# Attention by pairs of heads in the halves of TensorE's rows

## The chip, the cores and the metric

The kernel runs on one core of a Trainium2 chip. The metric is the device time of one execution in microseconds. Engines are named as the profile names them: PE (TensorE, matmuls), PEld (its weight loads), DVE (VectorE), ACT (ScalarE), POOL (GpSimd) and SP (SyncE, which issues nearly all DMAs).

## What is computed

Three layers follow each other. Attention with a sigmoid in place of the softmax: 4 batches, 12 heads, 448 tokens, 64 values per head. Then a dense block with 768 inputs and 2048 hidden values (ELU). Then a mixture of 8 experts, in which a greedy assignment gives each expert 224 tokens.

```
scores = scale * np.matmul(q, k.transpose(0, 1, 3, 2)) - np.log(S)
attn = 1.0 / (1.0 + np.exp(-scores))
x = np.matmul(attn, v)                      # (4, 12, 448, 64) -> rows of 768
h = x @ w_in
x2 = np.where(h > 0.0, h, np.exp(np.minimum(h, 0.0)) - 1.0) @ w_out
logits = x2 @ w_gate                        # greedy choice, 224 tokens an expert
out[mask] = np.maximum(x2[mask] @ w1[e], 0.0) @ w2[e]
```

## The kernel before

**Precision.** Most matmuls work on float32r operands that are split in two: a high part (a copy that rounds, `hcopy`, on ACT or DVE) and a low part (the rest, a subtraction on DVE, `lsub`). A product is then high by high, high by low and low by high: three matmuls, one "group of three". Products with v are plain float32 matmuls; the trace shows each as two MATMUL instructions.

**Attention** (`attention`, L452). For each head the host lays k and q transposed and twice below each other: 64 rows and the same 64 rows again. `prep` (L442) makes `kk`, whose upper half is the high part of k and whose lower half the low part, and `qh` and `ql`, the high and the low part of q in both halves. One matmul of `kk` with `qh` over all 128 rows then gives high by high and low by high at once, a second one with `ql` the rest: two matmuls of 448 columns per head and chunk of 112 keys. The result lies in one of three PSUM banks (`sc`); ACT applies the sigmoid, one instruction per head and chunk, into one of eight tiles `s`. Products with v follow four (head, chunk) steps later, in one unit per chunk in batch 0 (`AC0`) and per two chunks later (`AC1`): the two heads of a pair write partitions 0 to 63 and 64 to 127 of one bank (`av`). After four chunks the pair's output is split into `xH` and `xL`, one tile each for the six pairs of a batch.

**Dense block.** `layer1` (L496) makes 16 tiles of hidden values, each with six groups of three into one of four banks (`mm`), and then the epilogue: exp and tanh on ACT, two DVE operations that read the bank, and the split into `gH` and `gL`. `layer2` (L519) makes six output tiles of 16 groups of three each, in the first three of these banks; the fourth (`lg`) collects the logits. `rows_out` (L575) transposes a finished tile in an `sc` bank and stores it. In batch 0 the weights come as wide integers, and `weights` (L417) turns them into float32 with three DVE operations and one of ACT before the split; later batches read the copy that it has stored.

**Order.** A planner (`Plan`) writes the whole order before the kernel runs. Every operation has a cost and a rank by place in the program; the planner takes, engine by engine, what can start first, and the lower rank among ties. Units (`plan.unit`) of matmuls stay together. Work that depends on data waits for the ends that the planner has computed; on the chip each engine keeps this order. The program order is attention 0, then for each batch `layer1(b)`, `attention(b + 1)`, `layer2(b)`. A sigmoid needs another table of ACT than exp and tanh, and the planner counts 1.3 us for a change.

After the dense block come the search (counting matmuls and DVE operations in `search`), the lists, gathers and the experts, which use all eight banks under new names.

Of the kernel before, what the change touches and what calls it, by code (L numbers as in the profile page):

```python
# [18 lines left out]
MM = 4  # L19
PC = 1  # L20
XLA = 4
NK = 4
NA_ = 8
AV = 7
PP = 2
NR = 3
# [26 lines left out]
class Plan:  # L53
# [39 lines left out]
    @staticmethod  # L93
    def region(ap):
        steps = list(ap.ap)
        size = mybir.dt.size(ap.dtype)
        name = ap.tensor.name
        if ap.tensor.__class__.__name__ == "Tile" and ap.space != bass.MemoryType.DRAM:
            if ap.space == PSUM:
                return name, 0, 128, 0, 2048  # L100
            row = steps[0][0]
            p0, off = divmod(ap.offset, row) if row else (0, ap.offset)
            span = 1 + sum((n - 1) * s for s, n in steps[1:])
            return name, p0, p0 + steps[0][1], off * size, (off + span) * size
        span = 1 + sum((n - 1) * s for s, n in steps)
        return name, 0, 1, ap.offset * size, (ap.offset + span) * size
# [180 lines left out]
def kernel(  # L287
# [11 lines left out]
    B, H, D2, S = kq.shape  # L299
    S, D = S // 2, D2 // 2  # L300
    NT, DM = out.shape
# [82 lines left out]
    xH = p1.tile([P, KD, S], F32R)  # L384
    xL = p1.tile([P, KD, S], F32R)
# [11 lines left out]
    heads = {}  # L397

    def load_head(h):
        if h >= B * H or h in heads:  # L400
            return
        b, hh = divmod(h, H)
        x = r_kq()
        if h == 0:
            for c in (slice(0, S), slice(S, 2 * S)):
                plan.dma(x[:, c], kq[b, hh][:, c])
        else:
            plan.dma(x, kq[b, hh])
        vr = None
        if hh % 2 == 0:  # L410
            vr = r_v()
            plan.dma(vr.rearrange("p c d -> p (c d)"), vP[b, hh // 2])
        heads[h] = (x[:, :S], x[:, S:], vr)
# [28 lines left out]
    def prep(h, st):  # L442
        kr, qr, vr = heads[h]
        kk, qh, ql = r_kk(), r_qh(), r_ql()
        hcopy(kk, kr)
        lsub(kk[D:], kr[D:], kk[D:])
        hcopy(qh, qr)
        lsub(ql, qr, qh)
        st[h] = (kk, qh, ql, vr)
        load_head(h + 2)  # L450

    def attention(b):  # L452
        st, ad = {}, {}
        n0, n1 = b * H * C, (b + 1) * H * C
        LA = XLA
        AC = AC0 if b == 0 else AC1

        def scores(n):
            g, r = divmod(n, 2 * C)
            c, j = divmod(r, 2)  # L460
            h = 2 * g + j
            if n < n0 + 2:
                prep(h, st)
            if c == PP + j and g + 1 < (b + 1) * (H // 2):
                prep(h + 2, st)
            kk, qh, ql, _ = st[h]
            ps = sc()
            with plan.unit():
                for i, m in enumerate((qh, ql)):
                    PE.matmul(ps[:CP, :S], kk[:, c * CP:(c + 1) * CP], m, start=i == 0, stop=i == 1)  # L470
            ad[n] = r_s()[:CP]
            A.activation(ad[n], ps[:CP, :S], AF.Sigmoid, bias=bias_s[:CP], scale=QS)

        for n in range(n0, n1 + LA):
            if n < n1:
                scores(n)
            m = n - LA
            if m < n0 or (m + 1) % (2 * AC):
                continue
            g, r = divmod(m, 2 * C)  # L480
            c = r // 2
            if c == AC - 1:
                ps = av()
            v = st[2 * g][3]
            with plan.unit():
                for i in range(AC):
                    for j in range(2):
                        o, k = slice(j * D, (j + 1) * D), c - AC + 1 + i
                        PE.matmul(ps[o, :S], v[:, k, o], ad.pop(m + 1 - 2 * (AC - i) + j), start=k == 0,
                                  stop=k == C - 1)  # L490
            if c == C - 1:
                hp = g % (H // 2)
                hcopy(xH[:, hp, :], ps[:, :S])
                lsub(xL[:, hp, :], ps[:, :S], xH[:, hp, :])

    def layer1(b):  # L496
        ws = {}
        for f in range(-2, KF):
            with plan.first(200), plan.after(xH[:, GW + f]) if b == 0 and f < 1 else nullcontext():
                if f + 2 < KF:  # L500
                    ws[f + 2] = weights(b, f + 2)
# [4 lines left out]
            for c in range(KD):  # L506
                with plan.unit():
                    for n, (w, m) in enumerate(((h, xH), (h, xL), (l, xH))):
                        PE.matmul(ps[:, :S], w[:, c, :], m[:, c, :], start=c == 0 and n == 0,
# [9 lines left out]
    def layer2(b):  # L519
        ws = {}  # L520
        m3 = Ring(banks[:MM - 1])

# [7 lines left out]
        for d in range(KD):  # L530
# [10 lines left out]
            x2, xh, xl = r_s() if b == B - 1 else r_x2(), r_x2h(), r_x2l()  # L541
            last = b == B - 1 and d == KD - 1
            with plan.first(3000):
# [11 lines left out]
                if d == KD - 1:  # L555
# [3 lines left out]
                    pl = sc()[:, :(j1 - j0) * 2 * E]  # L559
# [15 lines left out]
    def rows_out(b, d, x2, e):  # L575
        rows, pr = r_rows(), sc()
# [7 lines left out]
    load_head(0)  # L584
    load_head(1)
# [119 lines left out]
    def search(parts, n=1):  # L705
# [8 lines left out]
        for i, (nb, sh) in enumerate(BITS):  # L714
# [33 lines left out]
            if lead:  # L748
                warm(W1, banks[3], full[:K])
# [30 lines left out]
    mm, sc, av = Ring(banks[:3]), Ring(banks[3:7]), Ring(banks[7:])  # L780
# [24 lines left out]
    def listing(ph):  # L805
# [8 lines left out]
        if ph == 0:  # L814
            warm(W4, banks[3], csb)
# [19 lines left out]
        if ph == 0:  # L835
            warm(W3, banks[3], idx)
# [167 lines left out]
```

## Time and profile before

| | before |
|---|---|
| median of three runs | 1052.14 us (1050.41 to 1054.1) |
| profiled execution | 1051.52 us |
| its span, first to last instruction | 1049.6 us |
| mean granted clock of PE in it | 0.973 |
| attention 0 and layer 1 of batch 0 | 0 to about 149 us |
| layer 2 of batch 0, attention 1 | about 149 to 250 us |
| batches 1 to 3 | about 250 to 700 us |
| search and experts | from about 700 us |

The span is what the rows below count from. Matmuls are pipelined: the start of one to the start of the next is what it costs, its own duration is longer. A mean of a group is of one instruction.

### The profile page before, as it was taken

Reading aid. Unit: us, or ns where it says so; the run is one execution under the profiler, and the core shown is the slowest. Engines: PE = TensorE matmul, PEld = TensorE weight load, DVE = VectorE, ACT = ScalarE, POOL = GpSimd, SP = SyncE. Lnnn points to the kernel's source line nnn. Section 1 sums busy time; section 2 is a strip of 40 time slices with the busy share of each in tenths; the row PEclk is TensorE's granted clock in tenths of the full one; section 3 lists DMA queues with packets and bytes.
Section 4 is the critical chain, followed back from the end, with each engine's and each line's share of the span. In section 5 each row is a group of like instructions: output and inputs, shape, how many; then the busy total and the mean of one; then the engine's idle time right before and its main releaser. Section 6 shows DMA issues by size and latency. Waiting matters only on the chain. (4 is left out here: it accounts for less than half of the span.)

```text
span 1049.6 us, 15479 instructions
## 1 busy us (share of the span) xinstructions
PE 997.6 (95%) x5810; PEld 837.4 (80%) x5810; DVE 752.7 (72%) x1446; ACT 453.2 (43%) x790; POOL 44.5 (4%) x43
## 2 busy tenths in 40 slices
PE   8998879999999999999999999978969999999997
PEld 3466755789985788995698999955969999899997
DVE  5878987867885545995244995448788898898871
ACT  5887657743357402347412331024244453353330
POOL 0000000000000000000000000001021121020200
PEclk9998989999999999999999999996989999999999
DMA  6785766664335433334133333126255375375830
GB/s 204 266 299 211 231 242 257 202 238 147 114 125 178 138 117 103 111 132 156 29 113 102 106 126 104 58 53 236 108 217 203 146 239 203 120 266 193 296 100 26
DMA packets 54058, 170.89 MB, mean 163 GB/s; under 512 B 6112, under 2 KB 17120, under 8 KB 52448
## 3 DMA queue, kind: packets, MB, share of 16 engines
q1 hardware_dynamic: 51424, 158.90, 44.4%
q0 software_dynamic: 2560, 11.01, 3.3%
q8 instruction: 45, 0.74, 0.3%
q14 instruction: 29, 0.24, 0.1%
HBM read 146.30 MB, written 23.59 MB: 162 GB/s over the span
## 5 line engine op out<-in xcount | busy, mean ns | idle before, releaser
L246 PE MATMUL bank<-xH,wh 128*128 128x448 f32 x384 | 143.6, 374 | 11.1 <-DVE a L246 9.9
L246 PE MATMUL bank<-x,eh 128*128 128x224 f32 x768 | 141.4, 287 | 5.9 <-ACT x L246 3.2
L246 PE MATMUL bank<-gH,wh 128*128 128x448 f32 x384 | 142.1, 370 | 0.0
L246 PE MATMUL bank<-xL,wh 128*128 128x448 f32 x384 | 141.7, 369 | 0.0
L246 PE MATMUL bank<-xH,wl 128*128 128x448 f32 x384 | 141.5, 369 | 0.0
L246 PE MATMUL bank<-gH,wl 128*128 128x448 f32 x384 | 140.6, 366 | 0.0
L246 PE MATMUL bank<-gL,wh 128*128 128x448 f32 x384 | 140.4, 366 | 0.0
L246 PEld LDWEIGHTS bank<-x,eh 128*128 128x128 f32 x768 | 120.8, 197 | 8.0 <-ACT x L246 3.7
L246 DVE TENSOR_TENSOR wl<-wd,wh 128x768 fp32r<-128x768 f32 (+1 forms) x112 | 119.6, 1070 | 9.4 <-ACT wh L246 4.6
L246 DVE TENSOR_TENSOR el<-eraw,eh 128x768 fp32r<-128x768 f32 x128 | 121.0, 950 | 3.7 <-ACT eh L246 2.9
L246 ACT ACTIVATE s<-bank,bias_s 112x448 f32<-112x448 f32 x192 | 110.6, 635 | 28.0 <-PE bank L246 24.4
L246 DVE CAST wh<-wd 128x768 fp32r<-128x768 f32 (+1 forms) x83 | 51.3, 618 | 91.9 <-PE bank L246 88.7
L246 ACT ACTIVATE eh<-eraw 128x768 fp32r<-128x768 f32 x106 | 85.9, 842 | 70.1 <-DMA eraw<-we 57.8
L246 ACT ACTIVATE a<-bank 128x448 f32<-128x448 f32 x128 | 66.1, 541 | 105.8 <-PE bank L246 99.5
L246 PE MATMUL bank<-x,el 128*128 128x224 f32 x384 | 107.0, 279 | 0.0
L246 PEld LDWEIGHTS bank<-xH,wh 128*128 128x128 f32 x384 | 73.1, 190 | 23.2 <-issue 10.8
L246 PE MATMUL bank<-eh,hH 128*112 128x384 f32 x256 | 88.6, 346 | 0.0
L246 PE MATMUL bank<-eh,hL 128*112 128x384 f32 x256 | 86.3, 337 | 0.0
L246 PE MATMUL bank<-el,hH 128*112 128x384 f32 x256 | 86.2, 337 | 0.0
L246 PE MATMUL bank<-s,vr 112*64 112x448 f32 x384 | 84.5, 557 | 0.0
L246 PE MATMUL bank<-qh,kk 128*112 128x448 f32 x192 | 75.8, 395 | 8.1 <-DVE kk L246 6.6
L246 PEld LDWEIGHTS bank<-gH,wh 128*128 128x128 f32 x384 | 72.2, 188 | 11.0 <-issue 3.5
(143 smaller groups left out, 1597.1 us busy)
## 6 DMA issues: line engine op xcount, KB each, us to landing
eraw<-we SPq DMA_DIRECT2D x64, 768.0 KB, 5.3
kq<-kq SPq DMA_DIRECT2D x47, 448.0 KB, 4.0
wd<-wcopy SPq DMA_DIRECT2D x48, 384.0 KB, 2.9
wd<-wcopy SPq DMA_DIRECT2D x36, 512.0 KB, 3.2
arena<-w_in SPq DMA_DIRECT2D x16, 768.0 KB, 5.3
arena<-w_out SPq DMA_DIRECT2D x12, 1024.0 KB, 8.4
wcopy<-wd SPq DMA_DIRECT2D x16, 384.0 KB, 4.9
wcopy<-wd SPq DMA_DIRECT2D x12, 512.0 KB, 4.2
```

Source lines behind the costliest of these rows:

```text
L246: fn = lambda: getattr(self.eng[e], name)(*args, **kw)
```

## The change

Pairs of heads take the place of single heads. The host lays the two heads of a pair below each other (64 rows each), so that k and q are loaded once and not twice. `prep` splits a pair with one copy and one subtraction over 896 columns (k and q side by side). The scores of a chunk are a group of three for each head, each over 64 rows: head 0 in rows 0 to 63, head 1 in rows 64 to 127, taken in turn; they go to the two banks of a "twin" tile, and one sigmoid reads both. PSUM has two twins, one `av` bank and three `mm` banks (four before); `layer2` has two of these (three before), and the logits have the third. From batch 1 on, the scores of two chunks and the products with v of the two chunks before them are one unit ("one stretch"); in batch 0 they stay apart. The output of a pair goes to a ring of nine tiles each for the high and the low part. The costs of the planner follow the new shapes, and PSUM regions are told apart by bank, as a twin has two.

```diff
-MM = 4
+MM = 3
-XLA = 4
-NK = 4
-NA_ = 8
-AV = 7
+XLA = 2
+NK = 2
+NA_ = 4
+XT = 3
...
-            if ap.space == PSUM:
-                return name, 0, 128, 0, 2048
...
+            if ap.space == PSUM:
+                return name, 0, 128, off // 512, (off + span + 511) // 512
...
-            if ins[0].dtype == F32R and out.shape[0] == 64:
-                return 0.121
+            if ins[0].dtype == F32R and ins[0].shape[0] == 64:
+                return 0.104
...
-    banks = [psum.tile([P, 512], F32, name=f"bank{i}") for i in range(8)]
-    mm, sc, av = Ring(banks[:MM]), Ring(banks[MM:AV]), Ring(banks[AV:])
+    banks = [psum.tile([P, 512], F32, name=f"bank{i}") for i in range(4)]
+    twins = [psum.tile([P, 2, 512], F32, name=f"twin{i}") for i in range(2)]
+    mm, sc, av = Ring(banks[:MM]), Ring(twins), Ring(banks[MM:])
...
-    r_v = ring(p1, "vr", [CP, C, P], F32, 3)
-    r_kk = ring(p1, "kk", [P, S], F32R, NK)
-    r_qh = ring(p1, "qh", [P, S], F32R, NK)
-    r_ql = ring(p1, "ql", [P, S], F32R, NK)
+    r_v = ring(p1, "vr", [CP, C, P], F32, 4)
+    r_kqh = ring(p1, "kqh", [P, 2 * S], F32R, NK)
+    r_kql = ring(p1, "kql", [P, 2 * S], F32R, NK)
-    r_s = ring(p1, "s", [P, S], F32, NA_)
+    r_s = ring(p1, "s", [P, 2, S], F32, NA_)
...
-    xH = p1.tile([P, KD, S], F32R)
-    xL = p1.tile([P, KD, S], F32R)
+    r_xH = ring(p1, "xH", [P, S], F32R, KD + XT)
+    r_xL = ring(p1, "xL", [P, S], F32R, KD + XT)
+    xs = [[] for _ in range(B)]
...
-    def prep(h, st):
-        kr, qr, vr = heads[h]
-        kk, qh, ql = r_kk(), r_qh(), r_ql()
-        hcopy(kk, kr)
-        lsub(kk[D:], kr[D:], kk[D:])
-        hcopy(qh, qr)
-        lsub(ql, qr, qh)
-        st[h] = (kk, qh, ql, vr)
-        load_head(h + 2)
+    def prep(g, st):
+        x, vr = pairs[g]
+        h, l = r_kqh(), r_kql()
+        for c in (slice(0, S), slice(S, 2 * S)) if g == 0 else (slice(0, 2 * S),):
+            hcopy(h[:, c], x[:, c])
+            lsub(l[:, c], x[:, c], h[:, c])
+        st[g] = (h[:, :S], l[:, :S], h[:, S:], l[:, S:], vr)
+        load_pair(g + 2)
...
         def scores(n):
+            g, c = divmod(n, C)
+            kh, kl, qh, ql, _ = st[g]
             ps = sc()
+            for i, (w, m) in enumerate(((kh, qh), (kh, ql), (kl, qh))):
+                for j in range(2):
+                    o = slice(j * D, (j + 1) * D)
+                    PE.matmul(ps[:CP, j, :S], w[o, c * CP:(c + 1) * CP], m[o], start=i == 0, stop=i == 2)
+            return ps
+
+        def values(n):
+            g, c = divmod(n, C)
+            if c == 0:
+                acc[g] = av()
+            v, s = st[g][4], ad.pop(n)
+            for j in range(2):
+                o = slice(j * D, (j + 1) * D)
+                PE.matmul(acc[g][o, :S], v[:, c, o], s[:, j], start=c == 0, stop=c == C - 1)
+
+        for n in range(n0, n1 + XLA, AC):
+            new = [i for i in range(n, n + AC) if i < n1]
+            old = [i for i in range(n - XLA, n - XLA + AC) if i >= n0]
...
             with plan.unit():
+                pss = [scores(i) for i in new]
+                if b:
+                    for i in old:
+                        values(i)
+            if not b and old:
+                with plan.unit():
+                    for i in old:
+                        values(i)
+            for i, ps in zip(new, pss):
+                ad[i] = r_s()[:CP]
+                A.activation(ad[i], ps[:CP, :, :S], AF.Sigmoid, bias=bias_s[:CP], scale=QS)
...
+                h, l = r_xH(), r_xL()
...
-    mm, sc, av = Ring(banks[:3]), Ring(banks[3:7]), Ring(banks[7:])
+    mm, sc, av = Ring(banks[:3]), Ring([t[:, i] for t in twins for i in range(2)]), Ring(banks[3:])
...
+    kt, qt = (x.transpose(0, 1, 3, 2).reshape(B, H // 2, 2 * D, S) for x in (k, q))
...
-        "kq": np.concatenate([dup(k), dup(q)], axis=3), "vP": vp,
+        "kq": np.concatenate([kt, qt], axis=3), "vP": vp,
```

The warm-up matmuls of the search move from the fourth bank to the third, which is then the logits' one, and layer 2 of the last batch keeps its six results in three of the double `s` tiles.

## Rows read from the trace of the kernel before

**Rows 1.** The page's totals: busy us (share of the span) xinstructions.

```profile
PE 997.6 (95%) x5810; PEld 837.4 (80%) x5810; DVE 752.7 (72%) x1446; ACT 453.2 (43%) x790; POOL 44.5 (4%) x43
```

**Rows 2.** Busy time by stretch: us, each engine (instructions), clock, DMA, GB/s.

```profile
0.00:12.70 12.70, 7.73 (x23) 3.81 (x23) 7.24 (x29) 5.64 (x9) 0.43 (x5) 0.92 0.71 200
12.70:82.00 69.30, 68.72 (x301) 37.74 (x300) 50.99 (x78) 53.89 (x95) 0.00 (x0) 0.99 0.78 271
82.00:93.00 11.00, 6.29 (x17) 4.70 (x17) 9.76 (x16) 10.30 (x18) 0.00 (x0) 0.69 0.88 313
93.00:109.50 16.50, 16.50 (x81) 14.86 (x80) 14.47 (x23) 11.67 (x21) 0.00 (x0) 1.00 0.40 133
109.50:149.00 39.50, 28.81 (x129) 24.73 (x128) 35.47 (x51) 22.30 (x35) 0.00 (x0) 0.91 0.70 240
149.00:250.00 101.00, 99.87 (x494) 77.06 (x493) 74.42 (x108) 60.08 (x94) 0.62 (x3) 1.00 0.64 223
250.00:600.00 350.00, 350.00 (x1722) 287.14 (x1722) 226.05 (x378) 138.21 (x254) 0.00 (x0) 1.00 0.37 117
```

The engines in these rows are PE, PEld, DVE, ACT and POOL. Eleven of the 23 matmuls before 12.7 us are warm-up matmuls ahead of the first scores.

**Rows 3.** Timeline of PE in attention 0: start, us, what, xcount.

```profile
31.32 0.46 PE L246 MATMUL bank<-qh,kk 128*112 128x448 f32 x1
31.61 0.37 PE L246 MATMUL bank<-ql,kk 128*112 128x448 f32 x1
31.91 0.97 PE L246 MATMUL bank<-s,vr 112*64 112x448 f32 x4
32.81 0.46 PE L246 MATMUL bank<-qh,kk 128*112 128x448 f32 x1
...
47.19 1.72 PE L246 MATMUL bank<-s,vr 112*64 112x448 f32 x8
```

**Rows 4.** Timeline of PE at the start; in brackets the idle time before.

```profile
4.73 0.43 PE L246 MATMUL bank<-qh,kk 128*112 128x448 f32 x1
...
9.57 0.46 PE L246 MATMUL bank<-qh,kk 128*112 128x448 f32 x1 [3.40 <-DVE kk L246]
```

**Rows 5.** Timeline of PE from 82 to 149 us.

```profile
85.30 0.45 PE L246 MATMUL bank<-qh,kk 128*112 128x448 f32 x1 [3.21 <-DVE kk L246]
...
143.39 0.71 PE L246 MATMUL bank<-xH,wh 128*128 128x448 f32 x1 [5.23 <-DVE a L246]
```

**Rows 6.** Groups by shape, whole span: xcount, busy us, mean ns, idle before.

```profile
L246 ACT ACTIVATE s<-bank,bias_s 112x448 f32<-112x448 f32 x192 | 110.6, 635 | 28.0 <-PE bank L246 24.4
L246 PE MATMUL bank<-s,vr 112*64 112x448 f32 x384 | 84.5, 557 | 0.0
...
L246 PE MATMUL bank<-ql,kk 128*112 128x448 f32 x192 | 71.8, 374 | 1.4 <-DVE ql L246 1.3
...
L246 DVE TENSOR_TENSOR wl<-wd,wh 128x768 fp32r<-128x768 f32 x64 | 61.1, 955 | 5.0 <-ACT wh L246 2.0
L246 DVE TENSOR_TENSOR wl<-wd,wh 128x1024 fp32r<-128x1024 f32 x48 | 58.6, 1222 | 4.4 <-ACT wh L246 2.6
...
L246 DVE TENSOR_TENSOR ql<-kq,qh 128x448 fp32r<-128x448 f32 x48 | 29.9, 624 | 1.1
L246 DVE TENSOR_TENSOR kk<-kq,kk 64x448 fp32r<-64x448 f32 x48 | 29.9, 623 | 3.1 <-ACT kk L246 1.7
...
L246 ACT ACTIVATE wh<-wd 128x768 fp32r<-128x768 f32 x18 | 15.1, 845 | 10.9 <-PE bank L246 10.9
...
L246 ACT ACTIVATE wh<-wd 128x1024 fp32r<-128x1024 f32 x11 | 11.6, 1057 | 12.5 <-PE bank L246 9.0 <-DVE wd L246 3.5
```

**Rows 7.** Timeline of PE in the expert stage, two places three weight loads apart.

```profile
861.08 0.27 PE L246 MATMUL bank<-x,el 128*128 128x224 f32 x1
...
861.41 0.28 PE L246 MATMUL bank<-x,el 128*128 128x224 f32 x1
```

**Rows 8.** DMA issues: xcount, KB each, us to landing.

```profile
kq<-kq SPq DMA_DIRECT2D x47, 448.0 KB, 4.0
```

**Rows 9.** Busy time by stretch, instructions that touch `xH` alone.

```profile
12.70:82.00 69.30, 15.87 (x48) 9.01 (x48) 3.73 (x6) 3.29 (x6) 0.99 0.78 271
```

More of the change, by code (lines that the diff above doesn't have):

```diff
@@ L395, with load_pair @@
     Lm = const.tile([P, NJ, E], F32)
-    heads = {}
-    def load_head(h):
-        if h >= B * H or h in heads:
+    pairs = {}
+    def load_pair(g):
+        if g >= B * HP or g in pairs:
             return
-        b, hh = divmod(h, H)
-        x = r_kq()
-        if h == 0:
+        b, hp = divmod(g, HP)
+        x, vr = r_kq(), r_v()
+        if g == 0:
             for c in (slice(0, S), slice(S, 2 * S)):
-                plan.dma(x[:, c], kq[b, hh][:, c])
+                plan.dma(x[:, c], kq[b, hp][:, c])
         else:
[L408 to L413, printed above, removed]
+            plan.dma(x, kq[b, hp])
+        plan.dma(vr.rearrange("p c d -> p (c d)"), vP[b, hp])
+        pairs[g] = (x, vr)
     wcopy = dram.tile([KF + 2 * KD, P, KH, P], F32, name="wcopy") if wide else None
@@ L452, in attention @@
     def attention(b):
         st, ad = {}, {}
-        n0, n1 = b * H * C, (b + 1) * H * C
-        LA = XLA
+        n0, n1 = b * HP * C, (b + 1) * HP * C
         AC = AC0 if b == 0 else AC1
+        acc = {}
         def scores(n):
[L459 to L466, printed above, removed]
-            ps = sc()
-            with plan.unit():
[L469 to L494, printed above, removed]
+            g, c = divmod(n, C)
@@ new lines, in attention @@
+        for n in range(n0, n1 + XLA, AC):
+            new = [i for i in range(n, n + AC) if i < n1]
+            old = [i for i in range(n - XLA, n - XLA + AC) if i >= n0]
+            for i in new:
+                g, c = divmod(i, C)
+                if i == n0:
+                    prep(g, st)
+                if c == PP and g + 1 < (b + 1) * HP:
+                    prep(g + 1, st)
+            with plan.unit():
+                pss = [scores(i) for i in new]
[9 more added lines that the diff above has]
+                A.activation(ad[i], ps[:CP, :, :S], AF.Sigmoid, bias=bias_s[:CP], scale=QS)
+            if old and old[-1] % C == C - 1:
+                h, l = r_xH(), r_xL()
+                ps = acc.pop(old[-1] // C)
+                hcopy(h, ps[:, :S])
+                lsub(l, ps[:, :S], h)
+                xs[b].append((h, l))
@@ L498, in layer1 @@
         for f in range(-2, KF):
-            with plan.first(200), plan.after(xH[:, GW + f]) if b == 0 and f < 1 else nullcontext():
+            with plan.first(200), plan.after(xs[0][GW + f][0]) if b == 0 and f < 1 else nullcontext():
                 if f + 2 < KF:
@@ L507, in layer1 @@
                 with plan.unit():
-                    for n, (w, m) in enumerate(((h, xH), (h, xL), (l, xH))):
-                        PE.matmul(ps[:, :S], w[:, c, :], m[:, c, :], start=c == 0 and n == 0,
+                    for n, (w, m) in enumerate(((h, 0), (h, 1), (l, 0))):
+                        PE.matmul(ps[:, :S], w[:, c, :], xs[b][c][m], start=c == 0 and n == 0,
                                   stop=c == KD - 1 and n == 2)
@@ L521, in layer2 @@
         m3 = Ring(banks[:MM - 1])
+        keep = [r_s() for _ in range(KD // 2)] if b == B - 1 else None
         def fetch(i):
@@ L575, in rows_out @@
     def rows_out(b, d, x2, e):
-        rows, pr = r_rows(), sc()
+        rows, pr = r_rows(), sc()[:, 0]
         with plan.unit() if b < B - 1 else nullcontext():
@@ L583 @@
     late = []
[L584 to L585 removed]
+    load_pair(0)
+    load_pair(1)
     V.memset(bias_s, -math.log(S))
@@ L748, in search @@
             if lead:
-                warm(W1, banks[3], full[:K])
+                warm(W1, banks[2], full[:K])
             V.tensor_reduce(out=num if last else dlt, in_=nums, axis=AX.X, op=ALU.max)
@@ L814, in listing @@
         if ph == 0:
-            warm(W4, banks[3], csb)
+            warm(W4, banks[2], csb)
         V.tensor_reduce(out=s2, in_=sp_.rearrange("p (x j) -> p j x", x=2), axis=AX.X, op=ALU.min)
@@ L835, in listing @@
         if ph == 0:
-            warm(W3, banks[3], idx)
+            warm(W3, banks[2], idx)
         xg = []
```

10 lines of the change are left out of this document (4 added, 6 removed).

## The prediction

> **What bounds the kernel now.** I read the totals first [rows 1]: TensorE is busy for 95% of the span, VectorE for 72%, ScalarE for 43%. A share over the whole span says little here, so the next view is busy time by stretch [rows 2]. Its stretches are cut where the work changes: the start (0 to 12.7 us), attention of batch 0 (to 82), the changeover to layer 1 of batch 0 (to 93), the rest of that layer (to 149), then layer 2 of batch 0 with attention of batch 1 (to 250). From 250 to 600 TensorE is busy for 350.0 of 350 us at full clock: whatever TensorE is spared there comes off the time, and what ScalarE or VectorE is spared does not, as they are busy for 138 and 226 us. Before 149 it is otherwise. From 93 to 109.5 us the rows show 81 matmuls in 16.5 us, 0.204 us each; that is the price of one 448-column float32r matmul at full clock. At this price the 12 score matmuls between the first one (4.73 us [rows 4]) and 12.7 are 2.4 us of work in 8.0, the 17 between 82 and 93 are 3.5 in 11, and the 129 from 109.5 to 149 are 26.3 in 39.5. The three stretches lose 5.5, 7.5 and 13.2 us: 26 us in which TensorE stands, or runs at the lower clock (means of 0.92, 0.69 and 0.91).
>
> The timeline says what it stood for. At the start it is the second head: the first has its scores by 6 us, the next score matmul waits 3.40 us for that head's `kk` [rows 4]. At 85.30 it is again `kk`, at 143.39 the layer-1 epilogue on VectorE (`a`, 5.23 us) [rows 5]. From 109.5 to 149 VectorE is busy for 35.5 of 39.5 us [rows 2]: the conversion of the weights of batch 0 and the epilogues set the pace there, not TensorE.
>
> **The scores.** There are 96 pair-chunks (4 batches, 6 pairs of heads, 4 chunks). Each now takes four matmuls over 128 rows (192 + 192 in all; [rows 6] has one half), 0.815 us. The change takes six over 64 rows, two at a time in the two halves. If the halves run side by side this is three times 0.204 = 0.611 us, a gain of 0.204 per chunk, 19.6 us for 96. If they run one after the other it is six times 0.204, a loss of 39.2 us. These are the two ends. No row shows row halves. The nearest are the products with v, whose outputs lie in the two column halves: each MATMUL has a mean of 557 ns against 374 for the float32r one [rows 6], yet four of them more in one stretch add only 1.72 - 0.97 = 0.75 us [rows 3], 0.19 each. So an instruction that streams for two passes (557 - 374 = 183 ns more, one pass) is issued every single pass: two are in flight at a time, in different halves. The weights don't forbid it: in the expert stage three loads of 128 columns are taken every 0.33 us (861.08 to 861.41 [rows 7]), 0.11 each, while six loads of 112 columns have 0.611 us here. I take the near end, -19.6 us, with a chance kept for the far one.
>
> The Trainium skill, "TensorE: Matmul & The Clock Gate", section "The mechanism", says that matmuls in different row groups overlap and start some 4 ns apart. By that figure, an estimate, 288 pairs would cost 1.2 us more; no run so far shows it.
>
> **The changes of mode.** A visit to the column halves isn't free. From the `qh` matmul at 31.32 to the next at 32.81 [rows 3] are 1.49 us; two score matmuls (0.41) and four value matmuls (0.75) leave 0.33 us for going in and coming out. In batches 1 to 3 this visit exists 36 times (12 per batch, two chunks each), before and after. What is new is a third change: layer matmuls, row halves, column halves, layer matmuls. Its cost is between 0 and a whole visit, 0.33 us; a half is nearest, 0.17, or 6.1 us for 36 (bounds 0 and 12). In batch 0, where scores and products with v alternate already, the row halves take the place of the full array on one side; where a layer-1 group stands between, a change is added. I take 1 us (0 to 4).
>
> This is where a rule speaks against the change. The Trainium skill, "TensorEngine Tiling (Array Packing)", section "Key Properties", says that changing the mode, not only the tile, drains TensorE. It gives no price; the 0.33 us above agree with it, and by it the third change is certain to cost something.
>
> **What the other engines are spared.** Splitting now takes, for each head, two subtractions of 0.62 us (48 each in the trace) and two copies; for a pair that is 2.5 us of VectorE for the subtractions alone. After, it is one subtraction over 896 columns: between 0.955 (768 columns) and 1.222 us (1024), so 1.09. Copies go from four to one, 0.95 us on ScalarE by the same interpolation of 0.845 and 1.057 [rows 6]. The sigmoid goes from 192 of 0.635 us to 96 over 896 columns; 448 more columns at the slope of those copies (0.83 ns) make 1.01 us, 0.26 less per chunk. From 149 on, a saturated TensorE hides all of it and I count nothing. Before 149 it counts through the 26 us:
>
> Start: pair 0 arrives in the two loads that head 0 took, so four chunks have their rows at once, and the second load (448 KB, 4.0 us to landing [rows 8]) is needed only for the next pair. I take back 4.5 of 5.5 us (bounds 2 and 5.5).
>
> 82 to 149: attention of batch 0 needs per pair about 1.4 us less of VectorE's subtractions and 1.0 us less of sigmoids, plus the copies, and so ends earlier (1.4 us for six pairs is 8.5 us of VectorE); the chain of conversions and epilogues behind it starts earlier. Besides, nine xH/xL tiles in place of six let three pairs of batch 1 be finished while layer 1 of batch 0 still reads its own six; now the second pair stands until that layer is through. So there is other work for TensorE in the holes. Against it: layer 1 has three banks for four. During attention 0 no epilogue runs, and the 24 groups of three that ran ahead (48 reads of `xH`, two a group [rows 9]) are exactly four banks of six groups; with three it is 18, so 3.7 us of filling are pushed back into the stretch with the holes. Also, sigmoids between exp and tanh need table loads on ScalarE. Of 20.7 us I take 11 as recovered (bounds 0 and 20.7), a half, as VectorE's own work from 82 to 149 stays near 60 us.
>
> **Edits counted at nothing.** Layer 2 has two banks for three: its next tile takes 48 matmuls, 9.8 us, and the previous bank is read by a copy of about 0.6 us, so a bank is free long before; without that cover each of 24 tiles would wait that copy. The ring of three doesn't divide 16 layer-1 tiles, so in batch 2 the first tile falls on the bank of the logits and waits for some three steps of 0.6 us; the second tile and attention 3 are ready to run instead. Two twins for three score banks: `rows_out` holds a twin for one copy, and layer groups fill. SP issues two loads per pair for three and nothing else is queued behind new waits. The bank renaming of the search and the experts moves no work.
>
> **The sum**, against the profiled 1051.5 us (span 1049.6, median of three runs 1052.1): -19.6 + 6.1 + 1 - 4.5 - 11 = -28.0, so 1023.5; I say **1024**.
>
> **The rivals.**
> *The row halves don't overlap.* The trace has column halves only, that is for it; the rate of weight loads is against it. Place: the scores; price 0.204 us for each of 576 matmuls, +39.2 in place of -19.6: 1082 us. It decides from the point where a pair of matmuls takes about 0.30 us (the other terms, -8.4 us, are then eaten), halfway between 0.204 and 0.408. Here the change is slower.
> *The holes stay.* VectorE sets the pace from 82 to 149, and three banks and table loads eat what splitting gave back: -19.6 + 7.1 - 2 = -14.5, 1037 us. For it: 35.5 of 39.5 us busy. Against it: VectorE has less to do.
> *The joined stretch waits.* It needs both twins empty and both older chunks through their sigmoids before its first matmul: 2.02 us of ScalarE behind a stretch of some 3.2 us (1.22 scores, 1.5 products, 0.5 changes). TensorE's order is fixed; an epilogue of 0.5 to 0.85 us in ScalarE's queue ahead of a sigmoid makes it late. At 0.78 us for each of 36 stretches the 28 us are gone: 1052. Against it: ScalarE is busy for only 138 of 350 us, and layer groups are put between.
>
> **Chances.** The forecast 0.62, with 1010 to 1040 as its own range (26 us recovered and no third change, 1006, is the far bound; 4 us recovered and 0.33 us a change, about 1040, the other). The holes stay 0.13 (1034 to 1044), the joined stretch waits 0.09 (1044 to 1062), no overlap 0.16 (1065 to 1085). The range 1009 to 1048 leaves out the last, part of the third and a little below. Faster by over 0.3% (3 us, about what a measurement here can tell): 0.62 + 0.13 + 0.03 = 0.78; within it 0.05; slower 0.02 + 0.15 = 0.17.
>
> **What will show it.** In the timeline of batches 1 to 3 the six score matmuls of a chunk should start within about 0.6 us, in close pairs; 1.2 us is the first rival. The gap at each change: 0.1 to 0.2 us. In the groups: 96 sigmoids near 1.01 us, some 25 splitting subtractions near 1.09. The first product with v well before 12.7 us; layer 1 of batch 0 ending some 20 us before 149; products with v of batch 1 ahead of that end. From 250 to 600 TensorE still without a wait; waits on `s` there would be the third rival. From 700 on nothing should differ but the start. The forecast is wrong if TensorE's work in that stretch doesn't shrink, or if the part before 149 doesn't.

## The result, and the profile after

The changed kernel takes 1038.8 us (median of four runs, 1037.3 to 1040.2), the kernel before 1053.1 on the same chip (four runs, 1050.4 to 1056.5): ratio 0.987 [0.983, 0.991], 1.3% faster. Forecast was 1024, a gain of 28 us; 14.3 came. The profiled execution took 1037.3 us with a span of 1035.5; against [rows 1] and the span before, 1049.6, that is 14.1 less, which is what the traces have to explain.

The totals after (engine, busy us, share of the span, instructions), beside [rows 1]: TensorE 10.5 us less, VectorE 26.6, ScalarE 37.1.

```profile
PE 987.1 (95%) x6002; PEld 820.0 (79%) x6002; DVE 726.1 (70%) x1364; ACT 416.1 (40%) x640; POOL 44.3 (4%) x43
```

Busy time by stretch, cut at the same places of the program in both: the end of layer 2 of batch 0, of batch 2 and of batch 3. Columns as in [rows 2]. The kernel before:

```profile
0.00:245.00 245.00, 222.91 (x1010) 158.75 (x1011) 189.55 (x298) 161.02 (x264) 1.05 (x8) 0.97 0.69 238
245.00:572.00 327.00, 327.00 (x1610) 265.94 (x1609) 206.08 (x339) 129.78 (x237) 0.00 (x0) 1.00 0.37 118
572.00:692.50 120.50, 120.50 (x596) 109.41 (x595) 75.77 (x120) 29.20 (x56) 0.00 (x0) 1.00 0.28 91
692.50:1049.00 356.50, 327.20 (x2600) 303.33 (x2599) 281.31 (x691) 133.17 (x235) 43.45 (x35) 0.95 0.51 177
```

The changed kernel:

```profile
0.00:228.00 228.00, 211.56 (x1101) 149.16 (x1102) 173.70 (x255) 140.98 (x182) 1.05 (x8) 0.98 0.68 228
228.00:552.00 324.00, 324.00 (x1711) 256.44 (x1711) 194.17 (x298) 114.09 (x170) 0.00 (x0) 1.00 0.33 104
552.00:675.00 123.00, 121.50 (x605) 109.57 (x603) 76.50 (x121) 28.36 (x56) 0.00 (x0) 1.00 0.27 89
675.00:1035.00 360.00, 330.08 (x2589) 304.81 (x2589) 281.73 (x691) 132.68 (x235) 43.23 (x35) 0.94 0.50 175
```

By the last matmuls of these stretches (244.5, 571.7, 692.5, 1042.8 before; 227.1, 551.7, 674.6, 1028.7 after) the lengths change by -17.4, -2.6, +2.1 and +3.7: sum -14.1. The first mark doesn't cut the work alike: the kernel before has run 98 of each of layer 1's three kinds of matmul ahead of it (96 of batch 0, two of batch 1), the changed one 96. These six matmuls (1.2 us) go over into the second stretch, so like for like the first two lengths change by -16.2 and -3.8. So the gain lies ahead of 228 us, the stretch without a wait gives little, and the end gives 5.9 back.

**The scores** did what was forecast. The timeline of PE at the start, beside [rows 4]:

```profile
5.46 0.47 PE L246 MATMUL twin<-kqh 64*112 64x448 f32 x2
...
8.23 0.97 PE L246 MATMUL bank<-s,vr 112*64 112x448 f32 x4
9.13 0.45 PE L246 MATMUL twin<-kqh 64*112 64x448 f32 x2
9.43 0.36 PE L246 MATMUL twin<-kql,kqh 64*112 64x448 f32 x2
9.63 0.36 PE L246 MATMUL twin<-kqh,kql 64*112 64x448 f32 x2
9.92 0.97 PE L246 MATMUL bank<-s,vr 112*64 112x448 f32 x4
10.83 0.46 PE L246 MATMUL twin<-kqh 64*112 64x448 f32 x2
```

Two matmuls start together, and the next two 0.20 us later: three such steps are 0.61 us. The first step takes 0.30, the last one 0.29 and the four products with v 0.91 where 0.75 is their work: the cycle from 9.13 to 10.83 is 1.70 us, 0.34 over 0.61 + 0.75, for two changes of mode, 0.17 each. The first score starts 0.73 us later than in [rows 4], the first product with v at 8.23 us; the second head's wait of [rows 4] is gone.

The groups by shape, beside [rows 6]; the two new sizes on the other engines (forecast 1.01 and 1.09 us) are there too:

```profile
L246 ACT ACTIVATE s<-twin,bias_s 112x896 f32<-112x896 f32 x96 | 92.7, 1006 | 84.7 <-PE twin L246 84.2
L246 PE MATMUL bank<-s,vr 112*64 112x448 f32 x384 | 83.6, 553 | 0.0
...
L246 DVE TENSOR_TENSOR kql<-kq,kqh 128x896 fp32r<-128x896 f32 x23 | 25.0, 1088 | 0.4
...
L246 ACT ACT_TABLE_LOAD x16 | 20.5, 1283 | 1.0 <-PEq L999 0.7
```

**The holes.** The waits of PE up to the end of layer 2 of batch 0 (us in total, times, the longest). The kernel before, to 245 us:

```profile
PE bank L246 <- DVE a L246: 9.9, 6, 5.2
PE bank L246 <- DVE kk L246: 6.6, 2, 3.4
PE bank L246 <- ACT s L246: 1.5, 3, 0.9
PE bank L246 <- DVE ql L246: 1.3, 2, 1.1
PE bank L246 <- ACT a L246: 1.2, 1, 1.2
...
```

The changed kernel, to 228 us:

```profile
PE bank L246 <- DVE a L246: 10.8, 5, 4.7
PE twin L246 <- ACT s L246: 2.2, 2, 1.7
PE bank L246 <- ACT wh L246: 1.6, 2, 0.9
PE bank L357 <- DVE idle L246: 1.2, 1, 1.2
PE bank L246 <- DVE wl L246: 0.6, 1, 0.6
```

The waits for split heads (`kk`, `ql`: 7.9 us) are gone, but those for the layer-1 epilogue (`a`) are as long as before, 10.8 against 9.9. All waits together fall from 21.9 to 16.4. The longest stands at 138.97, almost where [rows 5] has its own. The timeline of ACT ahead of it, with what an idle time before an instruction waited for in brackets:

```profile
121.26 1.28 ACT L246 ACT_TABLE_LOAD   x1
122.56 1.91 ACT L246 ACTIVATE s<-twin,bias_s 112x896 f32<-112x896 f32 x2
...
126.06 1.89 ACT L246 ACTIVATE s<-twin,bias_s 112x896 f32<-112x896 f32 x2
127.84 0.95 ACT L246 ACTIVATE kqh<-kq 128x896 fp32r<-128x896 f32 x1
131.92 1.14 ACT L246 ACTIVATE wd<-arena 128x1024 f32<-128x1024 f32 x1 [3.13 <-DMA arena<-w_out]
132.96 1.05 ACT L246 ACTIVATE wh<-wd 128x1024 fp32r<-128x1024 f32 x1
134.03 1.28 ACT L246 ACT_TABLE_LOAD   x1
135.32 1.42 ACT L246 ACTIVATE a<-bank 128x448 f32<-128x448 f32 x3
```

and the timeline of PE behind it:

```profile
132.51 1.72 PE L246 MATMUL bank<-s,vr 112*64 112x448 f32 x8
138.97 0.74 PE L246 MATMUL bank<-xH,wh 128*128 128x448 f32 x1 [4.74 <-DVE a L246]
139.51 0.57 PE L246 MATMUL bank<-xL,wh 128*128 128x448 f32 x1
139.88 0.57 PE L246 MATMUL bank<-xH,wl 128*128 128x448 f32 x1
```

ScalarE loads the sigmoid's table and takes four sigmoids in two lots of two and a copy for the next pair of heads. Then it stands for 3.13 us, as the next instruction in its fixed order converts a weight of the second dense layer (`w_out`) that hasn't landed, and it doesn't come back to exp and tanh before 135.3; TensorE has run out of work that is ready by then. The matmuls behind the hole start 0.37 us apart in place of 0.20: after 4.74 us without a matmul TensorE restarts at the lower clock, 1.2 GHz (granted 0.50; columns as in [rows 2]):

```profile
138.97:142.00 3.03, 3.03 (x8) 2.73 (x9) 3.00 (x5) 2.51 (x5) 0.00 (x0) 0.50 1.00 331
```

VectorE, which the prediction held to set the pace, stands idle itself for 1.88 us before 133.1, behind ScalarE's half of the same conversion. The hole of [rows 5] in the kernel before has the same load behind it; the timeline of ACT there:

```profile
138.25 1.12 ACT L246 ACTIVATE wd<-arena 128x1024 f32<-128x1024 f32 x1 [3.53 <-DMA arena<-w_out]
```

**Two new waits** lie behind. The timeline of PE at the start of layer 2 of batch 3, and (below the dots) in the last expert:

```profile
612.89 0.47 PE L246 MATMUL bank<-gH,wh 128*128 128x448 f32 x1 [0.69 <-ACT wh L246]
...
614.15 0.47 PE L246 MATMUL bank<-gH,wl 128*128 128x448 f32 x1 [0.58 <-DVE wl L246]
...
1014.84 0.33 PE L246 MATMUL twin<-eh,hL 128*112 128x384 f32 x1
1015.82 0.43 PE L246 MATMUL twin<-eh,hH 128*112 128x384 f32 x1 [0.65 <-DVE y L246]
```

Before, layer 2 of batch 3 follows layer 1 within 0.01 us. Now its first bank is the one that layer 1's sixteenth tile (16 = 5 x 3 + 1) has just filled, so the planner begins with the second tile, whose weights are being split. In the expert, two outputs lie in the halves of one twin; the first matmul of the one waits for the copy of the other.

### The profile page after: what moved, and what is told of

It reads as the page before. It is cut to its first block, busy times and chain, and to the rows that moved or that the text cites. A ratio compares the mean times of both kernels' runs of the same rounds, so it can differ in the third digit from the quotient of the medians.

```text
span 1035.5 us, 15477 instructions
## 1 busy us (share of the span) xinstructions
PE 987.1 (95%) x6002; PEld 820.0 (79%) x6002; DVE 726.1 (70%) x1364; ACT 416.1 (40%) x640; POOL 44.3 (4%) x43
## 5 line engine op out<-in xcount | busy, mean ns | idle before, releaser
L246 PE MATMUL bank<-xH,wh 128*128 128x448 f32 x384 | 144.5, 376 | 11.5 <-DVE a L246 10.8
L246 PE MATMUL bank<-gH,wh 128*128 128x448 f32 x384 | 144.3, 376 | 1.6 <-ACT wh L246 1.6
L246 DVE TENSOR_TENSOR wl<-wd,wh 128x768 fp32r<-128x768 f32 (+1 forms) x112 | 119.6, 1070 | 16.4 <-ACT wh L246 10.9
L246 ACT ACTIVATE s<-twin,bias_s 112x896 f32<-112x896 f32 x96 | 92.7, 1006 | 84.7 <-PE twin L246 84.2
L246 PEld LDWEIGHTS bank<-gH,wh 128*128 128x128 f32 x384 | 72.1, 188 | 26.2 <-issue 15.5
L246 PE MATMUL twin<-eh,hH 128*112 128x384 f32 x256 | 88.8, 347 | 1.5 <-DVE y L246 1.3
L246 PE MATMUL twin<-eh,hL 128*112 128x384 f32 x256 | 86.3, 337 | 0.0
L246 PE MATMUL twin<-el,hH 128*112 128x384 f32 x256 | 86.1, 336 | 0.0
L246 PEld LDWEIGHTS bank<-xH,wl 128*128 128x128 f32 x384 | 73.4, 191 | 6.7 <-DVE wl L246 0.3
```

Of the source, the lines that this page charges most:

```text
L246: fn = lambda: getattr(self.eng[e], name)(*args, **kw)
```

## The experiments

All edits are to the changed kernel, but for `e7_banks`. Ratios are to the kernel before, measured beside it. Ends of stages are the last matmul of each in the profile. A theory with a letter is stated in the expectation that uses it; the one that stood at the end is that of the lumps: scores and products with v of two chunks in one stretch make the work too coarse to fill the holes.

**1. Do the halves of the rows run side by side by the way they are issued?** `e6_order` issues all three matmuls of one head, then those of the other:

```
-            for i, (w, m) in enumerate(...):
-                for j in range(2):
+            for j in range(2):
+                for i, (w, m) in enumerate(...):
```

> The changed kernel with the six score matmuls of a chunk ordered by head (three for rows 0 to 63, then three for rows 64 to 127) and not in turn. If two matmuls run side by side only where neighbours in the order lie in different halves: a chunk takes about five steps of 0.204 us (only the third and fourth overlap) in place of three, 1.0 us and not 0.61; 96 chunks cost 39 us more, of which the holes before 144 us hide some: the span is 28 to 39 us longer, slower than the kernel before the change. If the halves overlap whatever the order: the same within 2 us.

Measured: 1036.9 us (1035.8 to 1037.4), ratio 0.987 [0.984, 0.991]: no difference. The timeline of PE:

```profile
30.43 0.47 PE L246 MATMUL twin<-kqh 64*112 64x448 f32 x2
30.72 0.38 PE L246 MATMUL twin<-kql,kqh 64*112 64x448 f32 x2
30.92 0.37 PE L246 MATMUL twin<-kqh,kql 64*112 64x448 f32 x2
31.23 1.72 PE L246 MATMUL bank<-s,vr 112*64 112x448 f32 x8
```

The starts are still pairs, one matmul of each head, although the program has three of one half ahead of three of the other. Of the two cases of the expectation the second came: the halves don't need to be issued in turn. It also settles the first rival.

**2. Does VectorE set the pace before 149 us?** `e5_conv` drops one of three conversions per wide weight (the sign):

```
-            V.scalar_tensor_tensor(out=di, in0=pr[:, :, :, 1], scalar=-0x80000000, in1=di, ...)
```

> This kernel is the changed one with one of VectorE's three operations per weight conversion of batch 0 left out (0.95 or 1.22 us each, 28 of them; the weights of the dense block lose their sign, the rest is computed as it is). Theory A, VectorE sets the end of layer 1 of batch 0 (it is busy for 81.8 of 93.8 us from the end of attention 0 to that end): the 18 or so conversions before that end spare 17 to 20 us of VectorE, the end moves from 144 us to 130 to 135, TensorE's waits for the epilogue (10.8 us) go below 4, and the span gets 7 to 12 us shorter. Rival B, three banks and table loads set it: the waits for the epilogue stay above 8 us and the span changes by less than 3 us.

Measured: 1034.7 us (1032.9 to 1036.7), 0.985 [0.981, 0.988]. Layer 1 of batch 0 ends at 125.2 in place of 144.1, but layer 1 of batch 1 at 282.8 for 287.4: of 19 us at the one mark 4.6 are left at the next, as what TensorE had done in between was work of attention 1, and that it now has to do later. The gain, 4.1 us by the medians, lies between the two theories (7 to 12, and under 3), and so do the waits for `a`, 6.7 us to the end of layer 2 of batch 0: VectorE's conversions have a part in the holes, but they alone do not set the time.

`e8_bias` raises VectorE's handicap when the planner chooses the engine for a copy, in the first group of work:

```
-BIAS = [{"V":.2},{"V":2.5},{"V":.8}]
+BIAS = [{"V":1.5},{"V":2.5},{"V":.8}]
```

> The changed kernel with the planner's handicap for VectorE raised from 0.2 to 1.5 us in attention of batch 0, so that the copies of that stretch (13 of k and q, 6 of the outputs of pairs, 0.62 us each on VectorE in the changed kernel) go to ScalarE. Theory A: 8 to 10 us of VectorE's work less before 51 us, so weights are converted earlier; layer 1 of batch 0 ends 3 to 6 us earlier, the span 2 to 5 us shorter. Rival: ScalarE, busy for 30.4 of 45.7 us there, is made the slower one: attention 0 ends 2 to 4 us later and nothing is gained.

Measured: 1040.7 us (1040.0 to 1041.6), 0.990 [0.986, 0.993]; attention 0 ends at 55.1 (51.3 in the changed kernel), layer 1 at 147.7. No gain: the balance of the two engines was not it either.

**3. The banks.** `e1_m3` starts layer 2 of batches 0 and 3 on the other bank:

```
-        m3 = Ring(banks[:MM - 1])
+        m3 = Ring(banks[:MM - 1] if b in (1, 2) else banks[MM - 2::-1])
```

> The changed kernel with the two banks of layer 2 taken in the other order in batches 0 and 3, so that the first tile of layer 2 doesn't fall on the bank of the sixteenth tile of layer 1. If the shared bank makes the stall at the start of layer 2 (0.94 + 0.58 us of waits at 145 us, 0.69 + 0.58 at 613 us): both go, the first group of layer 2 starts within 0.2 us of the last one of layer 1, the span is 2 to 4 us shorter. If it is the split of the weights that is late anyway: the waits stay and the span is the same within 1 us.

Measured: 1030.8 us (1028.1 to 1036.3, six runs), 0.981 [0.978, 0.984]. Layer 2 of batch 3 follows layer 1 at once and the two stages end 60.7 us apart in place of 62.8; from the end of layer 1 of batch 0 to that of batch 1 are 141.0 us in place of 143.3. That is 4.4 us, two stalls found and removed. The medians differ by 8.0, but the two intervals just overlap; what goes beyond 4.4 I leave to the scatter of these runs.

`e7_banks` gives the kernel before three banks for layer 1 and two for layer 2:

```
-MM = 4
+MM = 3
```

> The kernel before the change with three banks for layer 1 and two for layer 2, as in the changed one (the fourth goes to the scores, four banks). If three banks cost what the prediction gave them and the shared bank stalls at the start of layer 2: 18 groups and not 24 run ahead before the first epilogue, the holes grow by about 3.7 us, two stalls of 2 us are added, the span is 4 to 8 us longer than before the change. If a bank more for the scores makes up for it, or banks don't matter: within 2 us.

Measured: 1066.9 us (1063.9 to 1068.0), 1.015 [1.011, 1.019], 15 us slower. The marks say where: +4.9 at the end of layer 1 of batch 1, +7.8 at the end of layer 2 of batch 3, +13.1 at the first gather and +16.6 at the last matmul. What comes after the +7.8 I put down to the experiment and not to the question: the warm-up matmuls of the search use the fourth bank, which here is one that `rows_out` still uses. That is read from the code, and no run shows it. What banks cost the kernel before is then 5 to 8 us, with a fourth bank for the scores.

`e10_two` takes one more bank from layer 1:

```
-    mm, sc, av = Ring(banks[:MM]), Ring(twins), Ring(banks[MM:])
+    mm, sc, av = Ring(banks[:MM - 1]), Ring(twins), Ring(banks[MM:])
```

> The changed kernel with two banks for layer 1 in place of three. With two, 16 tiles end on the second bank and layer 2 begins on the first, so the stall at the start of layer 2 goes too (4.4 us in two batches, as the other order of layer 2's banks showed). If the number of banks sets how much of layer 1 runs ahead in attention 0 and so the holes: 12 groups run ahead and not 18, the waits for the epilogue before 145 us rise from 10.8 to 16 us or more, and the span is 0 to 6 us longer in all. If the number of banks matters only through the shared bank at the start of layer 2: the waits stay near 11 us and the span is 3 to 5 us shorter.

Measured: 1047.0 us (1041.5 to 1050.5, ten runs), 0.996 [0.994, 0.998]: 8 us slower than the changed kernel. Its waits of PE to 225 us:

```profile
PE bank L246 <- DVE a L246: 19.9, 9, 3.1
PE twin L246 <- ACT s L246: 2.6, 3, 1.6
...
```

The wait for the epilogue doubles (10.8 with three banks), and the loss is larger than the 0 to 6 us expected. The number of banks does reach the time.

**4. Tiles, lumps, tables.** `e4_six` takes back the ring of nine (`-XT = 3`, `+XT = 0`):

> The changed kernel with six tiles in the ring of outputs of pairs in place of nine. If running ahead into batch 1 fills the holes of layer 1 of batch 0: products with v of batch 1 ahead of the end of that layer fall from 12 chunks to 4, the holes grow from 11.5 us to 16 or more, and the span gets 6 to 10 us longer. If the holes are filled by something else, or VectorE is slowed by running ahead as much as TensorE gains: within 2 us of the changed kernel.

Measured: 1039.5 us (1039.3 to 1041.9), 0.990 [0.986, 0.993], 0.7 us above the changed kernel: three more tiles were worth nothing that can be measured there, although a score matmul of attention 1 waits 5.8 us for a sigmoid at 134.57.

`e3_apart` puts scores and products with v in units of their own in all batches:

```
             with plan.unit():
                 pss = [scores(i) for i in new]
-                if b:
-                    for i in old:
-                        values(i)
-            if not b and old:
+            if old:
                 with plan.unit():
```

> The changed kernel with scores and products with v of batches 1 to 3 in units of their own, as in batch 0. If each change of mode costs 0.185 us and joining saves one of four per stretch: from 288 to 552 us two batches show about 96 changes in place of 74, 2 us more there, and the span is 3 to 6 us longer. If the planner puts the two units side by side anyway, or gains from the freedom: the same within 1 us or up to 3 us shorter.

Measured: 1033.8 us (1030.6 to 1035.3), 0.982 [0.979, 0.986], against 0.987 [0.983, 0.991]: the intervals overlap. In batches 2 and 3 the planner lays the units side by side anyway: from the end of layer 2 of batch 0 to that of batch 2 are 324.7 us, with 324.6 in the changed kernel. The join saves nothing there. Layer 1 of batch 1 ends at 282.7 in place of 287.4.

`e9_tables` computes layer 1's two functions with the sigmoid, so that no table is loaded:

```
-            A.activation(e, ps[:, :S], AF.Exp)
-            A.activation(t, ps[:, :S], AF.Tanh, scale=0.5)
+            A.activation(e, ps[:, :S], AF.Sigmoid)
+            A.activation(t, ps[:, :S], AF.Sigmoid, scale=0.5)
```

> The changed kernel with sigmoid in place of exp and tanh in the epilogue of layer 1 (the hidden values are other ones; sizes and order of operations stay), so that ScalarE never changes its table. VectorE's part was nearly ruled out: with a conversion step less it has about 18 us less to do before the end of layer 1, and the dense block ended only 2 to 5 us earlier. Theory C, changes of table and the work held back by them leave the holes: the 16 table loads go (7 of them, 9.0 us of ScalarE, between 51 and 145 us), the waits for the epilogue there (10.8 us) fall below 5, layer 1 of batch 1 ends 4 to 7 us earlier (287.4 in the changed kernel's profile, 285.4 in two others of the same order). Rival: the holes come from three banks and the order alone, the waits stay above 8 us and the end within 2 us.

Measured: 1034.1 us (1032.1 to 1037.3), 0.984 [0.982, 0.986]. The waits for `a` fall from 10.8 to 2.3, but 5.0 for `s` and 2.3 for `xL` take their place: 4.7 us by the medians.

**5. The end of the last expert.** `e2_sc` lets neighbouring outputs lie in different twins:

```
-    ... Ring([t[:, i] for t in twins for i in range(2)]) ...
+    ... Ring([t[:, i] for i in range(2) for t in twins]) ...
```

> The changed kernel with the four banks of the experts' second layer taken from the twins in turn (half 0 of both, then half 1 of both) in place of both halves of one twin. If the two halves of a twin are kept apart only by the planner, and the wait in the program is for the tile as a whole: the two waits for the copy of y in the last expert (1.3 us in all) go, the last expert's second layer takes 16.6 us as before the change and not 18.4, the span is 1.5 to 2 us shorter. Rival: the wait is that of the copy itself, or the loss comes from the clock: no change.

Measured: 1040.3 us (1035.8 to 1042.8, six runs), 0.990 [0.987, 0.994]. The last expert's second layer takes 16.7 us, as before the change, in place of 18.5; but the earlier experts now wait 1.8 us for `y` on ScalarE in place of 0.2. Nothing net. `e11_last` therefore does it in the last expert alone, on top of `e1_m3`:

```
+        if ph == E - 1:
+            ys = [ys[0], ys[2], ys[1], ys[3]]
```

> The changed kernel with the other order of layer 2's banks in batches 0 and 3, and with the second layer of the last expert alone taking the twins in turn. The first was worth 4.4 us between layer marks (2.3 at 145 us, 2.1 at 613 us). For the second: taken in turn in all experts, the last expert's second layer took 16.7 us in place of 18.5, but waits for the copy of y came up in the experts before it (1.8 us in place of 0.2). If a twin is tracked as a whole, in the last expert alone it gives 1.8 us and costs nothing: 6 us less than the changed kernel in all, 1031 to 1034 us. If the waits come back elsewhere: 4.4 us less.

Measured: 1031.4 us (1028.4 to 1031.9), 0.980 [0.978, 0.982]. The last expert's second layer takes 16.7 us, 1.8 less; the median is that of `e1_m3`, so in the time of the whole it can't be told.

**6. Put together.** `e12_all` is `e11_last` with the units apart as in `e3_apart`:

> As the run before it, and scores and products with v in units of their own in batches 1 to 3 too. Alone that took 4 to 5 us from the part before 283 us and nothing from 283 to 547 us, where the planner laid the two units side by side anyway. If the stalls are separate they add up: 10 us less than the changed kernel, 1027 to 1030 us. If the units of their own had taken the same idle time as the banks' order (0.94 + 0.58 us at the start of layer 2 of batch 0 were gone there as well): 7 to 8 us less, 1030 to 1032.

Measured: 1023.1 us (1022.3 to 1025.3), 0.974 [0.972, 0.975], the fastest with the computation whole, and 8.3 us below `e11_last`, whose interval it doesn't touch. Its waits of PE to 215 us:

```profile
PE bank L246 <- DVE a L246: 5.5, 5, 1.9
PE bank L357 <- DVE idle L246: 1.2, 1, 1.2
PE twin L246 <- ACT s L246: 1.0, 2, 0.5
```

7.7 us in place of 14.6 in `e11_last` and 16.4 in the changed kernel. Layer 1 of batch 1 ends at 273.8 (284.7 in `e11_last`), 10.9 us earlier, and from there on the two run nearly alike: the whole gain of the smaller units lies before.

`e13_all_six` is `e12_all` with `XT = 0`:

> The version with units of their own and both bank orders, with six tiles in the ring of outputs of pairs in place of nine. In the joined kernel nine tiles were worth 1 us or nothing. Theory D, it is the lumps that kept the holes open (a joined unit needs both twins free and two sigmoids done before its first matmul, and brings 3.2 us at a time), and running ahead in small units fills them: then six tiles take the filling away, the idle time of TensorE before layer 1 of batch 1 rises by 5 us or more, and the time goes from 1023 to 1028 us or more. Rival: layer 2 of batch 0, whose first bank is free now, does the filling, and the number of tiles doesn't matter: 1021 to 1025 us.

Measured: 1028.5 us (1026.0 to 1034.1), 0.977 [0.973, 0.982]: 5.4 us slower by the medians, and no run of the one as fast as any of the other. Waits of PE of 12.8 us to 215 in place of 7.7, 2.8 of them for `xL`. So the three tiles do fill holes, once the units are small.

`e14_all_tables` is `e12_all` with the functions of `e9_tables`:

> The version with units of their own and both bank orders, with sigmoid in place of exp and tanh in the epilogue of layer 1 (other hidden values, the same sizes and order), so that no table is changed. In the joined kernel this took 4 to 6 us. If table loads as such cost TensorE time: 3 to 6 us less here as well, 1017 to 1020 us, the waits for the epilogue (5.5 us) near 2. Theory D, table loads hurt only where a lump of two sigmoids stands between them and a full set of banks: within 2 us of 1023.

Measured: 1018.5 us (1015.3 to 1019.7), 0.968 [0.963, 0.973]: 4.6 us faster by the medians, with 3.9 us of waits. The table loads cost as much with small units (nine of them from 48 us to the end of layer 1 of batch 0) as with joined ones (seven), against the theory of the lumps, which had them hurt only there.

## Why the prediction was half right

The sum, term by term (us; the forecast's own terms against what the traces show):

| term | forecast | measured |
|---|---|---|
| scores, 96 x 0.204 | -19.6 | -19.6 |
| changes of mode, all batches | +7.1 | +8.5 |
| waits and low clock up to the end of layer 2 of batch 0 | -15.5 | -8.5 |
| start of layer 2, batch 3 | 0 | +2.1 |
| last expert | 0 | +1.8 |
| start of the search | 0 | +0.8 |
| not accounted for | | +0.8 |
| sum | -28.0 | -14.1 |

The third row: TensorE's idle time falls from 22.1 to 16.4 us in the first stretch of the two tables by stretch; its busy time falls by 11.4, of which 9.8 are scores and 1.2 the six matmuls that went over into the next stretch, less 2.5 us of added changes: what is left, 2.9, I put down to fewer matmuls at the lower clock. The starts bear that out: 44 layer matmuls before and 29 after, other than at waits and changes, are over 0.30 us from the next one, 3.3 us less in all.

**The scores** were right in mechanism and size: three steps of 0.20 us, whatever the order of issue. The Trainium skill, "TensorE: Matmul & The Clock Gate", section "The mechanism", lets matmuls in different row groups overlap; the trace agrees, with pairs that start together.

**The changes of mode** were right in size, 0.17 us, and short in number. Between 228 and 552 lie batches 2 and 3 alone, 24 of the 36 visits, for which 24 new changes or 4.1 us were forecast. There 44 changes became 74, 30 more, and what all starts take over 0.204 us a step and 0.19 a product grew by 6.0 us. Ahead of 228 us, in batches 0 and 1, 62 became 77, 2.5 us at 0.17; the forecast had 12 x 0.17 + 1 = 3.0 there. The Trainium skill, "TensorEngine Tiling (Array Packing)", section "Key Properties", says that a change of mode drains TensorE; the trace agrees, with that price. So of 9.8 us that the scores give between 228 and 552 all but 3.8 are eaten, and the six matmuls from the stretch before (1.2 us) make it the 2.6 of the marks.

**The start** was right: 10.97 us of 12.7 busy (7.73 in [rows 2]) and the 3.40 us wait of [rows 4] is gone; one of 0.49 us for a sigmoid is what is left there, and the later first score. In the 8.0 us from 4.73 on stand 15 steps of scores and 12 products with v (5.3 us) and six changes (1.0): about 1.5 us are lost where 5.5 were, so some 4 came back of the 4.5 forecast.

**The failed step is "Of 20.7 us I take 11 as recovered"** for 82 to 149 us, with its reason, "as VectorE's own work from 82 to 149 stays near 60 us". With some 4 of the 8.5 us at the start, some 4.5 came back. Three things were wrong in it. First, I read the stretches by their time and not by their matmuls: attention of batch 0 ends at 61.7 us in the kernel before (51.3 after), and what ran to 82 was layer 1 and scores of batch 1. Secondly, the holes were of two kinds. Those for split heads went with the splitting, as forecast; those for the epilogue, which are the greater part, stayed (9.9 and 10.8 us). Thirdly, VectorE alone did not make them: a conversion taken out of every weight gave 4.1 us, no more than the table loads alone. I had read the hole of [rows 5] back to VectorE and no further; one step behind it, in both kernels, ScalarE waits for a weight's load (3.53 and 3.13 us), with the epilogue behind that conversion in its fixed order. No run moved that load, so what it is worth is open.

What the runs show in place of the 11 is that the holes hang on how much TensorE has at hand: one bank less costs 8 us, scores and products with v in units of their own give 8.3, the three tiles are worth 5.4 when units are small and nothing when they are joined, and table loads cost 4.6 to 4.7 with either. These prices overlap and are no sum. Why joined units keep the holes open stays open too. In `e12_all` the longest wait for `a` is 1.9 us, but ScalarE's longest wait for a load of `w_out` is 1.1 us there as well, so that run can't tell the lumps from the load.

**"Edits counted at nothing" failed twice.** "Layer 2 has two banks for three ... a bank is free long before" is true of its copies; what I left out is whose bank the first tile gets: in batches 0 and 3 it is layer 1's last. Turning the ring round gave 4.4 us, 2.3 of them inside the first stretch. And "the bank renaming of the search and the experts moves no work" is true of the work, but not of the waits: a twin is one tile to the program's bookkeeping of dependencies, so the neighbour's copy holds up a matmul that doesn't touch its half, 1.8 us in the last expert. The forecast that nothing changes behind 700 was wrong by 3.7 us; 1.1 of these, about the scatter between profiles of the gather and of the experts, stay open. Why the search starts 0.8 us later wasn't tried.

**The rivals.** No overlap (1082): refuted by the starts, and by `e6_order`. The holes stay (1037): this is nearest to what happened, and I gave it 0.13. That its number fits is luck in part: it had 2 us of waits recovered where 8.5 were, and none of the 4.7 us lost at layer 2 of batch 3, the search and the last expert. That banks and table loads reach the time is shown by `e10_two`, `e9_tables` and `e14_all_tables` (three banks against four only in the kernel before, by `e7_banks`); that VectorE alone sets the pace is not what happens. The joined stretch waits (1052): not at the 24 stretches of batches 2 and 3, as TensorE has no wait from 228 to 552; but in batch 1, next to layer 1 of batch 0, the join costs what `e12_all` gives back. That `e12_all` comes out at 1023, next to the forecast, is chance: the forecast had neither its edits nor its waits.

## What to carry to other kernels

Where one engine was saturated, the gain by rate arrived in full, but each new change of mode came off it: count the changes. Where the same engine has holes, ask for each hole what is waited for, what that engine waited for itself, and what else could be ready. Here buffers, banks and the size of units decided it, and the end of one stage moving by 19 us meant 4. When banks are counted anew, follow each ring across the stage boundary, and see which tiles share one buffer, before an edit is put at nothing.

## What the chip showed that was not expected

The two halves of the rows take their matmuls each by itself: issued in the order of heads, three and three, they start in pairs as when issued in turn (30.43, 30.72 and 30.92 us), and the time is the same (1036.9 and 1038.8). One of the two cases put down for that run had the order cost 28 us and more. The Trainium skill, in the section on the mechanism named above, has matmuls start strictly in the order of the program; the starts in this trace differ from that, and the measurement decides.
